# A linear-attention and channel-mix kernel rewritten on another tiling of its tokens

## The chip, the cores and the metric

The kernel runs on one core of one Trainium2 chip. A core has TensorE (matrix products, "PE"; its weight loads are listed apart as "PEld"), VectorE ("DVE"), ScalarE ("ACT"), GpSimd ("POOL") and SyncE ("SP"), which here only issues DMAs. The engines run side by side, each through its own list of instructions in order, and wait for each other by semaphores. SBUF is the working memory of 128 partitions, PSUM the memory that TensorE writes. The metric is the device time of one execution in microseconds (us), lower is better.

## What is computed

Four batches, four heads, 1,088 tokens, 32 features per head; r = 8. First an attention with a degree-2 sketch as its feature map, then a channel mix with d_model 128 and d_ff 1,024:

```python
def phi(x):                       # per token: 8 x 8 products
    a = np.einsum('rd,bhsd->bhsr', S1, x)
    b = np.einsum('rd,bhsd->bhsr', S2, x)
    return np.einsum('bhsi,bhsj->bhsij', a, b).reshape(*x.shape[:-1], r * r)
q_p, k_p = phi(q), phi(k)
kv = np.einsum('bhsf,bhsd->bhfd', k_p, v)
num = np.einsum('bhsf,bhfd->bhsd', q_p, kv)
den = np.einsum('bhsf,bhf->bhs', q_p, np.sum(k_p, axis=2))[..., None] + 1e-06
x = (num / den) with the heads side by side, (4, 1088, 128)

x_prev = x moved down by one token (zero first)
xk = mu_k * x + (1 - mu_k) * x_prev
xr = mu_r * x + (1 - mu_r) * x_prev
v = np.maximum(xk @ w_k, 0) ** 2 @ w_v
out = sigmoid(xr @ w_r) * v
```

Inputs and output are float32. The attention part is computed in float32, the channel mix in bfloat16 with float32 sums.

## The kernel before

A token is written 17 s + t, with s from 0 to 63 and t from 0 to 16. q, k and v of a batch are loaded by one DMA each from SP's queue (`load`, L120): two heads on the two halves of the 128 partitions, 64 values of s each, and for every partition and pair of heads 17 x 32 contiguous values. The weights come over GpSimd's queue (`w_load`, L215), two of them converted to bfloat16 by the DMA; mu_k and mu_r are loaded one value per partition.

Every task of the kernel is a small function, and one string, ORDER, lists them in the order in which they are issued; each engine takes its own instructions in that order. Numbers behind a name are batch or group, and part; a letter is the engine that does the copy or the product (A ScalarE, V VectorE). The tasks are:

- Attention, per batch, k side: transposes of k on TensorE (`t_pe`, L235) and their copies out of PSUM (`t_ev`); projections with S1 and S2 in four column strips of 32 (`kp_pe`, L252), their copy, and the 64 products per token and head (`kp_mul`, L273); sums over the tokens with v and of the projections themselves (`kv_pe`, L283), in 64-row tiles; their copy (`kv_cp`) and the forming of block-diagonal matrices (`kd_pe`, `kd_w`, `kd_ev`).
- Attention, per group of up to eight t (QG), q side: q is transposed in the same way; `q1_pe` (L355) projects it, together with a third product that gives the denominator; `q2` and `q2m` form denominator, quotient and the 64 products on VectorE; `q3_pe` and `q3_ev` transpose these; `q4_pe` (L408) multiplies by kv, which leaves x transposed (128 features by tokens) in PSUM.
- Channel mix: `q4_pp` writes (1 - mu_k) x to SBUF on ScalarE, `q4_xk` (L434) forms xk from it and from x in PSUM on VectorE, `q4_xb` writes x in bfloat16. `f1_pe` (L455) multiplies by w_k into two PSUM banks, `f1_act` is the relu on ScalarE (L464), `f1_sq` the square on VectorE (L470), `f2_pe` (L472) the product with w_v into the output's bank. `rr_pe` (L483) multiplies x and x_prev by w_r scaled by mu_r and by 1 - mu_r, two matmuls for every 128 tokens; `rr_act` is the sigmoid; `fin` (L498) the last product and the DMAs out.

Copies go through one helper, so in the profile they have the lines L196 (ScalarE) and L198 (VectorE), and are told apart by their tiles. Sixteen matmuls with zeros (L164) run at the very start. PSUM is given out by a pool with three names: two pairs of banks, three single banks and one for the output.

Of the kernel before, what the change touches and what calls it, by code (L numbers as in the profile page):

```python
# [64 lines left out]


# [482 lines left out]
```

## Time and profile before

| | us |
|---|---|
| runs | 119.43, 119.27, 117.3 |
| median of the runs | 119.27 |
| span of the profiled execution, first to last instruction | 115.9 |
| TensorE busy | 93.6 |
| TensorE weight loads busy | 72.1 |
| VectorE busy | 74.5 |
| ScalarE busy | 70.3 |
| GpSimd busy | 14.4 |

The profile shows the profiled execution by its span; its time as a run isn't listed beside it. The engine names in the rows are those given above, and a "q" behind one (SPq) is its instruction queue. A row of the list of groups reads: line, engine, operation, tile written <- tiles read, their shapes, how many; then busy us and mean ns of one; then how long the engine stood idle before them and who ended it. In the chain of waits (the work that ended last, followed back from the end), the three columns are the start, the length and what it was, with a count for consecutive ones. A row of sums by stage has the stage, its length, then for each engine busy us and number of instructions, then the clock that TensorE was granted as a share of full speed, the DMA engines' busy share and GB/s. Rows of the timeline have start, length, engine, line, operation and tiles.

### The profile page before, as it was taken

The numbers are of one execution on the slowest core, as the hardware profiler recorded it, in microseconds if no ns is written. First come the engines' busy times: TensorE is split into PE (matmuls) and PEld (weight loads), VectorE is DVE, ScalarE is ACT, GpSimd is POOL, SyncE is SP. The second block draws the span as 40 slices with busy tenths as digits, with TensorE's granted clock in tenths as the row PEclk, the third lists the DMA queues.
The fourth block names the chain that finished last, engine by engine and source line by source line (L and its number), as shares of the span: only waits on it lengthen the run. The fifth ranks groups of instructions, "written<-read, shape, count | busy, mean of one in ns | idle before, by whom it ended". The sixth has DMA issues, their size and how long they took to land.

```text
span 115.9 us, 5439 instructions
## 1 busy us (share of the span) xinstructions
PE 93.6 (81%) x2464; PEld 72.1 (62%) x2476; DVE 74.5 (64%) x149; ACT 70.3 (61%) x129; POOL 14.4 (12%) x47
## 2 busy tenths in 40 slices
PE   5995380794978996968877999899999999989820
PEld 2475270583867985667755888668858758667510
DVE  6128010269707939448637976979999999986820
ACT  4032230041629734737736997799999999999700
POOL 3059154000008000000002000100002300000000
PEclk9999999679999999999999999999999999999995
DMA  2999999900000000000020004021003011303213
GB/s 66 372 394 400 301 320 322 326 29 6 6 6 0 8 6 6 0 6 6 8 51 0 6 0 96 0 66 30 6 0 84 12 44 47 85 12 91 56 36 89
DMA packets 9317, 9.84 MB, mean 85 GB/s; under 512 B 1728, under 2 KB 6080, under 8 KB 9296
## 3 DMA queue, kind: packets, MB, share of 16 engines
q1 hardware_dynamic: 7984, 8.92, 24.1%
q0 software_dynamic: 1280, 0.59, 3.6%
q8 instruction: 19, 0.31, 1.1%
q14 instruction: 2, 0.02, 0.0%
q10 hardware_dynamic: 32, 0.00, 0.0%
HBM read 7.80 MB, written 2.23 MB: 87 GB/s over the span
## 4 chain that ended last, share of the span: by engine, by line
PE 73%; issue 13%; ACT 5%; DVE 3%; ACTq 1%; POOL 0%
PE o L479 11%; PE h L459 10%; PE x L416 9%; PE tp L243 8%; PE kv L294 7%; PE abw L366 6%; PE qt L399 6%; PE zeros L164 4%; PE abp L258 4%; PE r L491 3%; ACT k L464 2%; PE kv L301 2%; DVE kp L280 1%; ACTq L544 1%; PE kd L317 1%
## 5 line engine op out<-in xcount | busy, mean ns | idle before, releaser
L464 ACT ACTIVATE k<-h 128x1024 bf16<-128x1024 f32 (+1 forms) x36 | 35.0, 1002 | 1.8 <-PE h L459 1.2
L470 DVE TENSOR_TENSOR k<-k 128x1024 bf16<-128x1024 bf16 (+1 forms) x36 | 23.4, 656 | 2.2 <-ACT k L464 2.1
L479 PE MATMUL o<-wv,k 128*128 128x128 bf16 x272 | 20.8, 219 | 1.4 <-issue 0.7
L479 PEld LDWEIGHTS <-k 128*128 128x128 bf16 x272 | 17.1, 98 | 6.6 <-DVE k L470 1.4
L459 PE MATMUL h<-XK,wk 128*128 128x512 bf16 (+1 forms) x60 | 17.7, 364 | 1.0 <-DVE XK L438 0.4
L280 DVE TENSOR_TENSOR kp<-ab 128x1024 f32<-128x1024 f32 (+1 forms) x8 | 10.3, 1301 | 3.5 <-ACT ab L196 3.5
L301 PE MATMUL kv<-ab 64*32 64x16 f32 x272 | 9.5, 181 | 3.7 <-issue 3.7
L294 PE MATMUL kv<-kp,v 64*32 64x64 f32 x544 | 10.4, 225 | 2.0 <-DVE kp L280 1.2
L294 PEld LDWEIGHTS kv<-kp,v 64*32 64x32 f32 x544 | 8.5, 106 | 5.4 <-issue 3.1
L399 PE MATMUL qt<-ident,qp 128*128 128x128 f32 x68 | 10.6, 276 | 0.0
L393 DVE TENSOR_TENSOR qp<-an,abw 128x1024 f32<-128x1024 f32 (+2 forms) x9 | 10.4, 1159 | 0.1
L416 PE MATMUL x<-qpT,kvbd 128*32 128x256 f32 (+3 forms) x160 | 9.8, 351 | 0.8 <-issue 0.6
L301 PEld LDWEIGHTS kv<-ab 64*32 64x32 f32 x272 | 8.8, 106 | 1.9 <-issue 1.9
L429 POOL CAST XB<-X 128x63 bf16<-128x63 f32 x4 | 1.4, 343 | 64.2 <-ACT X L428 64.2
L366 PE MATMUL abw<-SQ,qT 128*32 128x96 f32 (+3 forms) x416 | 8.4, 228 | 1.0 <-issue 1.0
L432 ACT ACTIVATE PP<-x,omu_k 128x512 f32<-128x512 f32 (+7 forms) x12 | 6.7, 561 | 3.8 <-PE x L416 3.7
L366 PEld LDWEIGHTS abw<-SQ,qT 128*32 128x32 f32 x416 | 7.4, 116 | 2.3 <-issue 1.6
L399 PEld LDWEIGHTS qt<-ident,qp 128*128 128x128 f32 x68 | 7.7, 141 | 1.4 <-issue 0.2
L196 ACT COPY qpT<-qt 128x512 f32<-128x512 f32 (+2 forms) x15 | 8.4, 569 | 0.2 <-PE qt L399 0.2
L196 ACT COPY qT<-tp 128x512 f32<-128x512 f32 (+1 forms) x9 | 4.4, 494 | 6.4 <-PE tp L243 6.4
L438 DVE SCALAR_TENSOR_TENSOR XK<-x,mu_k,PP 128x512 bf16<-128x512 f32 (+7 forms) x12 | 6.8, 566 | 2.0 <-ACT PP L432 1.9
L198 DVE COPY kT<-tp 128x128 f32<-128x128 f32 (+1 forms) x5 | 2.2, 448 | 8.6 <-PE tp L243 8.6
(88 smaller groups left out, 142.2 us busy)
## 6 DMA issues: line engine op xcount, KB each, us to landing
k<-in_k_dram SPq DMA_DIRECT2D x4, 544.0 KB, 6.9
v<-in_v_dram SPq DMA_DIRECT2D x4, 544.0 KB, 10.3
q<-in_q_dram SPq DMA_DIRECT2D x4, 544.0 KB, 8.6
out_dram<-osb SPq DMA_DIRECT2D x11, 128.0 KB, 2.5
out_dram<-osb SPq DMA_DIRECT2D x4, 96.0 KB, 2.3
wk<-in_moe_w_k_dram POOLq DMA_DIRECT2D x1, 256.0 KB, 7.7
wv<-in_moe_w_v_dram POOLq DMA_DIRECT2D x1, 256.0 KB, 13.7
out_dram<-osb SPq DMA_DIRECT2D x4, 64.0 KB, 2.7
```

Source lines behind the costliest of these rows:

```text
L196: nc.scalar.copy(o, i)
L280: e.tensor_mul(kp[:, :n], _ap(a_, list(a_.ap[1:]) + [[0, R]]), _ap(b_, list(b_.ap[1:3]) + [[0, R]] + [b_.ap[3]]))
L294: nc.tensor.matmul(kv[32 * c:32 * c + 32, hh, :F], vin[b][rows, hp, t, :], kp[rows, t - t0, hp].rearrange("p i j -> p (i j)"), start=(t < ...
L301: nc.tensor.matmul(kv[32 * c:32 * c + 32, hh, F:F + 2 * R], ab[rows, t - t0].rearrange("p h x r -> p (h x r)"), ab[rows, t - t0, :, 1, :], ...
L366: nc.tensor.matmul(o[32 * c:32 * c + 32, i:i + n, hp, :] if n > 1 else o[32 * c:32 * c + 32, i, hp, :], xT["q", b][:, blk, 32 * c:32 * c + ...
L393: nc.vector.tensor_mul(qp[:, :n], _ap(a_, list(a_.ap[1:]) + [[0, R]]), _ap(b_, list(b_.ap[1:3]) + [[0, R]] + [b_.ap[3]]))
L399: nc.tensor.transpose(p[:, (i - 4 * hf) * P:(i - 4 * hf) * P + P], sb["qp", g][:, i].rearrange("p h i j -> p (h i j)"), ident[:])
L416: nc.tensor.matmul(p[32 * h:32 * h + 32, 64 * i0:64 * i1], kvbd[bs[i0]][:, hh, hp, :], r[:, i0:i1, 64 * hh:64 * hh + 64], skip_group_check ...
L459: nc.tensor.matmul(h[:, c, :n * 64], wk[:, (2 * cp + c) * P:(2 * cp + c + 1) * P], flat(XK, p0, n))
L464: nc.scalar.activation(k1[:, :, :n * 64], ps.pop(("h", g, cp))[:, :, :n * 64], RELU)
L470: nc.vector.tensor_mul(k2[:, :, :n * 64], k1[:, :, :n * 64], k1[:, :, :n * 64])
L479: nc.tensor.matmul(ps["o", g][:, i * P:i * P + P], k2[:, c, i * P:i * P + P], wv[:, 2 * cp + c, :], start=(cp == 0 and c == 0 and i == 0), ...
```

## The change

Nearly every task is rewritten, with the same mathematics:

- A token is written 34 a + u, with a from 0 to 31 and u from 0 to 33. The 128 partitions of q and k are now (head, a). Blocks of 32 x 32 are transposed on VectorE (`turn`), from SBUF to SBUF, which leaves (head, feature) on the partitions. Transposes of k and q on TensorE and their copies are gone.
- The projections take a whole 128 x 128 block of transposed tokens as the stationary operand (`kproj`, `abw`) and move block-diagonal S1 and S2. v is loaded in four pieces per batch, (u's quarter, a) on the partitions, and `kvmm` sums over 128 tokens at a time for each head.
- w_k, w_v and w_r are loaded in float32 on SP's queue and converted on GpSimd (`wset`); mu_k and mu_r are loaded as two rows and turned by a matmul. w_k and w_r are scaled by 1 - mu, and the mix becomes x mu / (1 - mu) + x_prev, so that x is copied out of PSUM once (`xev`), and r needs one matmul for 128 tokens instead of two; the r mix (`xr`) is done on GpSimd.
- Part of the k products (`kp.1.0`, `kp.3.0`, `kp.3.1`) and of the small products of the q side (`pw`, `an`) is on GpSimd; eight of the 36 squares are on ScalarE.
- Zero matmuls: five and five at the start, ten in seven places of the order (`zz`).
- PSUM is one tile of eight banks, and the order names the banks (behind @). The order itself is new throughout.

The core of the diff, without the removed functions:

```diff
+turn.k.0.0 wset.4 turn.k.0.1 wset.0 zz.1@0 kproj.0.1@0 kproj.0.0@1 abev.0.1.A turn.q.0.2 abev.0.0.A zz.2@0 zmm.0@0
+kp.0.1.V zev.0.A zz.1@7 wmm.0 wsq.0 kp.0.0.V zz.3@0 abw.0.1@0 abwt.0@1 abwev.0.1.A abw.0.0 turn.k.1.2 pw.0.18.34.G
+kvmm.0.0@0 abwev.0.0.A wset.1 kvmm.0.1 den.0.18.34 kproj.1.0@1 pw.0.0.18.G kvev.0.V an.0.18.34.G kproj.1.1@2
+den.0.0.18 abev.1.0.A kdmm.0 qp.0.1 abev.1.1.A an.0.0.18.G zz.1@1 zmm.1@1 kp.1.0.G zev.1.A qp.0.0 zz.1@7 wmm.1
+qt.0.1@23 qtev.0.1.A wsq.1 kvbm.0 zz.1@4 qtt.0@4 qt.0.0@56 kp.1.1.V qttev.0.A wset.3 xt.0 qtev.0.0.A kvmm.1.0@7
+turn.k.2.2 xmm.0.1@2 wset.2 xtev.0.A xs.0 turn.q.1.2 xmm.0.0@3 xev.0.1.A xr.0.2 kproj.2.1@5 xev.0.0.A xkt.0 turn.q.2.2
+abw.1.1@6 abev.2.1.A xr.0.0 abwt.1@5 abwev.1.1.A abw.1.0 xk.0.1 kproj.2.0@4 abwev.1.0.A xk.0.0 f1.1.1@01 xr.0.1
+abev.2.0.A kp.2.1.V rr.0@3 relu.1.1.A f1.0.0@56 zmm.2@2 kp.2.0.V kvmm.1.1 relu.0.0.A pw.1.0.34.G f1.1.0@01 rr.1@4
...
+    load_x(kin, k, 0, (slice(0, 1), slice(1, 2)))
+    load_x(qin, q, 0)
+    load_v(0)
+    load_x(kin, k, 1)
+    nc.sync.dma_start(wk_f[:, :, :DFF // 2], moe_w_k.rearrange("p (y f) -> p y f", y=2))
...
+    def turn(x, b, y):
+        n = U // 2 * D
+        for i in range(2):
+            if y in (i, 2):
+                if x == "k":
+                    nc.vector.transpose(_ap(kT[b % 2][:, 0, 2 * i], [[32, 2], [128, 9], [1, 32]]),
+                                        kin[b][:, i].rearrange("p (c m d) -> p c m d", c=2, m=9))
+                else:
+                    nc.vector.transpose(qT[b % 2][:, 17 * i:17 * i + 17, :].rearrange("p u a -> p (u a)"),
+                                        qin[b][:, i, :n])
+    def kproj(b, j, banks):
+        o = ps["ab", b, j] = PS[:, banks[0], :]
...
+            nc.tensor.matmul(_ap(d, [[n, 2], [1, 32]]), kT[b % 2][:, m].rearrange("p c a -> p (c a)"),
+                             SK[:].rearrange("p x h r -> p x (h r)"), skip_group_check=True)
+    def kvmm(b, j, banks=None):
...
+        for m in range(*KG[j]):
+            for h in range(H):
+                nc.tensor.matmul(o[32 * h:32 * h + 32, :F], vin[b][:, h, m, :],
+                                 sb["kp", b, j][:, 4 * (m - KG[j][0]) + h].rearrange("p i j -> p (i j)"),
+                                 start=(m == 0), stop=(m == 8), skip_group_check=True, tile_position=(0, 32 * h))
+    def xk(b, hf):
+        o = sb["xk", b, hf] = work.tile([P, 512], BF16, name="xk", tag="xk", bufs=4)
+        nc.vector.scalar_tensor_tensor(o[:], ps["x", b, hf], rat[:, :1],
+                                       X32[:, b % 2, 16 * hf:16 * hf + 16, :].rearrange("p u a -> p (u a)"),
+                                       op0=MUL, op1=ADD)
+    def xr(b, part):
...
+        nc.gpsimd.tensor_scalar(t[:, :n], x[:, u + 32:u + 32 + n], rat[:, 1:], 0.0, op0=MUL, op1=ADD)
...
+            nc.gpsimd.tensor_add(o[:], t[:], x[:, u:u + n])
+    def rr(g, banks):
...
+        for i in range(n):
+            nc.tensor.matmul(p[:, i * P:i * P + P], x[:, i * P:i * P + P], wr[:], skip_group_check=True)
     def fin(g):
...
+        for c in range(4):
+            rows = slice(32 * c, 32 * c + 32)
...
+            nc.sync.dma_start(dst, o[rows, :n // P, :])
```

The groups of the channel mix are now 512 tokens of one batch (16 values of u), two per batch, and a ninth one of 256 with the last two u of all four batches. `kdmm` is one transpose per batch, `zmm` and `wmm` give the denominator's weights, `qt` and `xmm` do what `q3_pe` and `q4_pe` did.

More of the change, by code (lines that the diff above doesn't have):

```diff
@@ L522 @@
+    for entry in ORDER.split():
+        task, _, banks = entry.partition("@")
+        name, *args = task.split(".")
+        args = [int(a) if a.isdigit() else a for a in args]
+        if banks:
+            args.append([int(i) for i in banks])
+        does[name](*args)
 _INS = ['q', 'k', 'v', 'S1', 'S2', 'moe_mu_k', 'moe_mu_r', 'moe_w_k', 'moe_w_v', 'moe_w_r']
```

679 lines of the change are left out of this document (303 added, 376 removed).

## The prediction

> **What bounds the kernel now.** I read the page's first line and its chain, then the list of the chain in order of time, then the sums by stage.
>
> ```profile
> PE 93.6 (81%) x2464; PEld 72.1 (62%) x2476; DVE 74.5 (64%) x149; ACT 70.3 (61%) x129; POOL 14.4 (12%) x47
> PE 73%; issue 13%; ACT 5%; DVE 3%; ACTq 1%; POOL 0%
> q8 instruction: 19, 0.31, 1.1%
> 12.74 1.99 issue
> 17.20 3.82 issue
> 27.44 1.73 issue
> 36.21 0.60 PE h L459 x4
> 110.93 0.69 DVE osb L502
> ```
>
> The chain that ended last runs through TensorE for 73% of the 115.9 us, and another 13%, 15.1 us, is "issue": the chain stands on an engine that waits for nothing the profile names. The other engines are on it for under 10%. The first matmul of the channel mix starts at 36.21, the last product ends at 110.93 + 0.69 = 111.62, and 4.2 us remain for the output to land.
>
> What the issue waits are is seen by counting TensorE's instructions up to each of the three longest:
>
> ```profile
> 0.00:12.74 12.74, 10.32 (x221) 6.35 (x222) 5.36 (x17) 3.83 (x8) 5.95 (x25) 1.00 0.85 312
> 0.00:17.20 17.20, 12.79 (x349) 8.53 (x349) 5.62 (x18) 5.06 (x10) 7.23 (x30) 1.00 0.92 308
> 0.00:27.44 27.44, 19.21 (x604) 13.89 (x604) 10.01 (x27) 7.11 (x16) 8.57 (x33) 0.94 0.84 268
> ```
>
> Matmuls and weight loads together make 443, 698 and 1208: 255 and 2 x 255 apart. The instruction queue moved 0.31 MB in 19 packets, and 4,940 TensorE instructions over 19 is 260. So I read the waits as TensorE coming to the end of a fetched block before the next is there; 15.1 us over 19 blocks is 0.8 us each. The kernel is bound by the number of TensorE's instructions as well as by their length.
>
> ```profile
> 36.20:60.00 23.80, 20.26 (x824) 16.79 (x829) 15.84 (x29) 13.41 (x28) 1.72 (x3) 1.00 0.03 8
> 60.00:80.00 20.00, 18.63 (x431) 14.99 (x429) 15.68 (x35) 16.94 (x33) 1.24 (x5) 1.00 0.13 31
> 80.00:105.00 25.00, 24.33 (x323) 17.59 (x326) 24.01 (x45) 24.33 (x38) 1.91 (x3) 1.00 0.15 35
> ```
>
> By stage (columns PE, PEld, DVE, ACT, POOL) TensorE is busy 85%, 93% and 97%; VectorE and ScalarE rise from 67% and 56% to 96% and 97%. So TensorE relieved alone gains in the first 80 us only; after that all three are full. The granted clock is 1.00 in all three.
>
> **TensorE after the change.** Rates from the chain, length over count:
>
> ```profile
> 80.14 0.44 PE qt L399 x4
> 79.69 0.45 PE o L479 x8
> 83.15 0.43 PE h L459 x2
> 84.83 1.07 PE x L416 x16
> 71.64 0.67 PE abw L366 x48
> 49.00 0.25 PE kv L294 x12
> 50.14 0.56 PE abp L258 x26
> 1.18 5.07 PE zeros L164 x16
> ```
>
> One f32 transpose is 0.11 us, an output matmul 0.056, a 512-wide one 0.215, an x instruction 0.067 at 256 columns, an abw 0.014, an abp 0.022; half a batch of kv, 96 instructions from 49.00 to 50.14, is 1.14, so 0.012 each. A plain f32 matmul shows as two instructions.
> - Gone: 72 transposes of k and q, 7.9; half of the 68 r matmuls, 1.9.
> - k projection: 320 instructions (6.9 us) become 72 with whole 128x128 weights. No row has this form; between the o row (0.056: 4.0) and the qt row (0.11: 7.9) I take 5, near the o row, as both move few columns.
> - kv and z: 816 (9.8) become 360 with four column strips. At the kv row 4.3, at twice that 8.6; I take 5.5.
> - q projection: 416 (5.8) become 96, 64 of them 96 wide; 5, an estimate by their columns.
> - kd: 192 become 12 instructions, about 2 to 0.9. x: 10 becomes 8.5. The qt transposes (7.5), f1 (14.7) and f2 (15.2) stay. Zeros: 16 become 20 (6.4 cold), the ten later ones in gaps.
>
> Sum, taken off the busy time: 93.6 becomes about 75, and 4,940 instructions become about 2,250: 9 blocks rather than 19, at 0.8 us 7 us of waits rather than 15. TensorE's line shrinks from 109 to 82 us, of which some 6 are zeros.
>
> **VectorE and ScalarE.**
>
> ```profile
> L470 DVE TENSOR_TENSOR k<-k 128x1024 bf16<-128x1024 bf16 x32 | 21.7, 685 | 2.2 <-ACT k L464 2.1
> L393 DVE TENSOR_TENSOR qp<-an,abw 128x1024 f32<-128x1024 f32 x7 | 8.5, 1218 | 0.0
> L502 DVE TENSOR_TENSOR osb<-o,r 128x512 f32<-128x512 f32 x8 | 5.5, 688 | 1.6 <-PE o L479 0.9 <-ACT r L496 0.7
> L438 DVE SCALAR_TENSOR_TENSOR XK<-x,mu_k,PP 128x512 bf16<-128x512 f32 x4 | 3.0, 744 | 0.0
> L198 DVE COPY qpT<-qt 128x512 f32<-128x512 f32 x3 | 2.0, 680 | 0.0
> L198 DVE COPY kT<-tp 128x128 f32<-128x128 f32 x3 | 0.9, 286 | 2.7 <-PE tp L243 2.7
> L464 ACT ACTIVATE k<-h 128x1024 bf16<-128x1024 f32 x32 | 32.8, 1051 | 1.8 <-PE h L459 1.2 <-PE x L416 0.3 <-PE kv L301 0.3
> L196 ACT COPY qpT<-qt 128x512 f32<-128x512 f32 x13 | 7.6, 596 | 0.2 <-PE qt L399 0.2
> ```
>
> The two copies give VectorE 154 ns + 1.03 ns per f32 element. The new VectorE transposes of 32x32 blocks stand in no row. I take the copy: 16 of 544 or 576 elements, 11.7 us; at the square's 0.5 ns 7, and at two passes 21 (an estimate: twice the copy's slope). [...]
>
> From the order: 28 squares on VectorE, four of them small, 18.2; 5 k products 6.6; 8 q products 10.2; xk and its tails 7.1; final products 5.9; 14 evictions 9.6; small ones, constants too, 10.2. With the transposes 79.5 us. Counted in this way (count times mean), before comes to 81.4, which overlap makes the 74.5 of the page; so 73 after. ScalarE keeps the 36 relus (36) and the sigmoids, takes 8 squares (8) and evictions, and loses PP, the copies of kT and qT and half of x: 67 against 81, so 59 busy against 70.
>
> **GpSimd.** It takes r's mix (24 instructions), 3 k products, part of the small products, and the scaling of the weights: about 16,000 elements per partition in 41 instructions.
>
> ```profile
> 17.92 0.39 POOL L233 COPY SQ<-SK 128x256 f32<-128x256 f32 x1
> 18.26 0.28 POOL L213 COPY klast<-k 128x128 f32<-128x128 f32 x1
> L229 POOL TENSOR_SCALAR wr_c<-wr_f,mu_r 128x128 bf16<-128x128 f32 x1 | 0.6, 609 | 0.1
> ```
>
> The copies give 0.9 ns an element and 0.17 fixed; the scaling, less the same 0.17, 3.4. So 21 to 61 us, and I take 2.1 ns, between them: 41 us, more than half idle. New waits hang on it. On VectorE den of batch 0 waits for a GpSimd product queued behind the scaling of w_k (1,024 elements, 1.1 to 3.7 us), and behind den wait qp and the turns of batch 2. On TensorE rr waits for xr, and f1 of a later group stands behind each rr. The five loads that leave its queue give 3 us back.
>
> **The front.** ```profile
> GB/s 66 372 394 400 301 320 322 326 29 6 6 6 0 8 6 6 0 6 6 8 51 0 6 0 96 0 66 30 6 0 84 12 44 47 85 12 91 56 36 89
> 0.73 0.44 SPq L123 DMA_DIRECT2D k<-in_k_dram  x1
> DMA to landing us min/median/max: 3.8/6.9/15.4
> ```
>
> SP's queue gets 28 loads instead of 12; at 0.44 us an issue that is 12.3 us, beside input that flows through the first eight of 40 slices, 23 us, and whose bytes don't change. q0 no longer stands behind v0. The first k lands 0.73 + 3.8 = 4.5 us in. Then VectorE in order: SK 5.6; two-part turn of k0, wset.4 and wset.0 to 8.6; q0 turned 10; two k products 12.8; turn of k1 14.3; den, the wait for the scaling 16.5; two qp 19.3; kp.1.1, turns of k2, q1, q2 25; xk 26.5. So f1 starts near 27, against 36.2: the two batches of turns are in it, the three issue waits and TensorE's transposes are not.
>
> **The sum.** By 27 VectorE has done 21 of its 73, so 52 remain; TensorE about 55 with its waits; ScalarE 51. Three nearly equal lines with GpSimd between them: before, the busiest engine was 92% busy from 36.2 to 105 (63.2 of 68.8). I take 85%, the lowest of the three stages: 61 us, so 88. Output 4.2, and 1 for the fourth DMA issue of the last products: span 93.5. The median of the runs, 119.27, stands 3.4 above the profiled span (the runs go from 1.4 to 3.6 above), and no time of the profiled execution itself is shown; I add 3.4: **97 us**. At 95% it is 90, at 75% 105.
>
> **Rivals.**
> 1. *VectorE and GpSimd shut each other out.*
>
> ```profile
> 36.20 1.29 POOL L213 COPY klast<-k 128x128 f32<-128x128 f32 x1
> 36.08 1.26 DVE L280 TENSOR_TENSOR kp<-ab 128x1024 f32<-128x1024 f32 x1
> 63.21 0.69 DVE L470 TENSOR_TENSOR k<-k 128x1024 bf16<-128x1024 bf16 x1
> 62.91 0.40 POOL L453 COPY XC<-XB 128x256 bf16<-128x256 bf16 x1
> ```
>
> A GpSimd copy of 0.28 takes 1.29 beside a product and ends 0.15 after it. The other way shows little: a square that starts 0.1 before a GpSimd copy ends takes its usual 0.69. If VectorE waits as well: 44 VectorE instructions with both inputs in SBUF meet a GpSimd that is busy 41 of some 77 us, half of a 1 us instruction each: 44 x 0.53 x 0.5 = 11.7 less what GpSimd yields, so +10: 107. [...]
>
> 2. *GpSimd becomes the bound (slower).* It starts near 11, waits some 10, then 41 x 0.17 + 16,000 p, then r, sigmoid, product 3, output 5.2, and 3.4. That is 39.6 + 16 p: over 121.7 from p = 5.1 ns, and 126 at 5.4. Against it: the dearest row is 3.4. For it: no f32 two-input row, and products with broadcast operands.
>
> 3. *The issue waits don't shrink* (it does not do what it says): blocks end at other places but cost the same 15.1 us: 8 on TensorE's line, 105.
>
> 4. *A tighter fit*: 95% or more, 90 or less.
>
> **How the numbers follow.** Forecast, 90 to 104: 0.56. Rival 1, 104 to 113: 0.20. Rival 2: 0.10. Rival 3: 0.06. Rival 4, down to 86: 0.08. The range 88 to 112 leaves out rival 2 and about half of rival 4, and takes in the dear end of the transposes (+9). No change means within 2%, 116.9 to 121.7, which is also about what a measurement of this kernel can tell. Faster 0.84 (all but rival 2 and the top of rival 1), within 0.05, slower 0.11.
>
> **What would show it.** Right: f1 starts near 27; transposes of 544 near 0.71; TensorE busy about 75 with some 2,250 instructions and issue under 8 us on the chain; VectorE above 80% from 27 on; chain spread over VectorE, ScalarE and TensorE. Wrong: squares and products beside GpSimd work stretched past their rows (rival 1); xr or the GpSimd k products at 3 us and rr waiting (rival 2); a start of f1 past 32.

## The result, and the profile after

| | before | after |
|---|---|---|
| runs, us | 119.43, 119.27, 118.2, 117.3 | 102.25, 102.22, 101.76, 104.45 |
| median, us | 118.73 | 102.23 |
| span of the profiled execution, us | 115.9 | 100.3 |

The ratio is 0.864, 95% interval 0.857 to 0.871: about 14% faster. The prediction was 97.0 with 88 to 112; the time is inside, 5.2 us above the point. The run of 104.45 was a disturbed one; such runs are left out of every ratio. The profiled execution is the one of 102.25, so 1.95 us lie around its span. Of the 15.6 us by which the span is shorter, 4.4 were won up to the first matmul of the channel mix, f1 (36.2 before, 31.8 after), and 12.9 from there to the end of the last product (75.4 before, 62.5 after); the output's tail lost 1.7 (4.3 before, 6.0 after).

The page of the changed kernel: busy times, the chain by engine, and the instruction queue.

```profile
PE 85.6 (85%) x1114; PEld 61.6 (61%) x1114; DVE 80.3 (80%) x128; ACT 60.4 (60%) x89; POOL 44.3 (44%) x70
q8 instruction: 8, 0.13, 0.5%
PE 30%; DMA 23%; DVE 23%; issue 9%; ACT 4%; POOL 3%; SPq 1%; DVEq 0%; POOLq 0%; ACTq 0%
```

TensorE has fallen from 73% of the chain to 30%, its instructions from 4,940 to 2,228, and the packets of the instruction queue from 19 to 8. Now the sums by stage (PE, PEld, DVE, ACT, POOL, then the granted clock), with the bounds that the prediction used for before:

```profile
10.00:20.00 10.00, 9.64 (x169) 7.50 (x169) 7.18 (x13) 2.59 (x7) 5.28 (x6) 1.00 1.09 248
20.00:27.00 7.00, 4.61 (x81) 2.55 (x78) 6.28 (x6) 3.15 (x6) 5.92 (x6) 1.00 1.08 266
27.00:36.20 9.20, 8.87 (x181) 7.07 (x182) 9.04 (x14) 6.02 (x12) 5.65 (x6) 1.00 0.81 178
36.20:60.00 23.80, 20.76 (x238) 15.49 (x232) 21.35 (x32) 20.11 (x27) 10.86 (x10) 1.00 0.09 25
60.00:80.00 20.00, 19.72 (x259) 14.02 (x258) 17.44 (x26) 13.73 (x19) 5.79 (x8) 0.92 0.10 28
```

From 27 us on no engine is the bound alone: VectorE is busy 98%, 90% and 87% of the three stages, TensorE 96%, 87% and 99%. Before, VectorE had 67% from 36 to 60. The chain changes engine all the time, which is what the small shares show.

**Where the 5.2 us of the miss lie.** Three rows of the timeline of the changed kernel (TensorE, VectorE, SP's queue) divide the span as the prediction had divided it:

```profile
31.77 0.59 PE L435 MATMUL ps<-xk,wk 128*128 128x512 bf16 x2
93.23 1.08 DVE L481 TENSOR_TENSOR osb<-ps,r 128x512 f32<-128x512 f32 x2
93.95 3.66 SPq L488 DMA_DIRECT2D out_dram<-osb  x8
```

| part | predicted | measured | difference |
|---|---|---|---|
| until the first f1 | 27 | 31.8 | +4.8 |
| from there to the end of the last product | 61 | 62.5 | +1.5 |
| to the end of the span | 5.2 (written as 5.5) | 6.0 | +0.5 |
| around the span | 3.4 | 1.95 | -1.5 |

The last product ends at 93.23 + 1.08 = 94.31. So nearly the whole miss of this execution is in the front; the same program, run again, had a front of 35.3 (next section). The second part came out close although two of its terms were off, as the next sections show.

### The profile page after: what moved, and what is told of

It is laid out like the page before. It is cut to its first block, busy times and chain, and to the rows that moved or that the text cites. A ratio compares the mean times of both kernels' runs of the same rounds, so it can differ in the third digit from the quotient of the medians.

```text
span 100.3 us, 2721 instructions
## 1 busy us (share of the span) xinstructions
PE 85.6 (85%) x1114; PEld 61.6 (61%) x1114; DVE 80.3 (80%) x128; ACT 60.4 (60%) x89; POOL 44.3 (44%) x70
## 4 chain that ended last, share of the span: by engine, by line
PE 30%; DMA 23%; DVE 23%; issue 9%; ACT 4%; POOL 3%; SPq 1%; DVEq 0%; POOLq 0%; ACTq 0%
DMA k<-in_k_dram 14%; DMA wk_f<-in_moe_w_k_dram 9%; DVE k L453 9%; PE ps L463 7%; PE ps L319 6%; PE ps L435 5%; PE ps L386 4%; ACT k L441 3%; DVE qp L355 2%; DVE qpT L224 2%; PE ps L245 2%; DVE xk L404 2%; PE ps L396 2%; PE ps L290 2%; POOL xrt L416 1%
## 5 line engine op out<-in xcount | busy, mean ns | idle before, releaser
L441 ACT ACTIVATE k<-ps 128x1024 bf16<-128x1024 f32 (+1 forms) x36 | 33.5, 984 | 2.6 <-PE ps L435 2.1
L463 PE MATMUL ps<-wv,k 128*128 128x128 bf16 x272 | 19.0, 219 | 2.1 <-DVE k L453 1.8
L435 PE MATMUL ps<-xk,wk 128*128 128x512 bf16 x64 | 17.7, 379 | 0.1
L355 DVE TENSOR_TENSOR qp<-an,abw 128x1024 f32<-128x1024 f32 (+1 forms) x8 | 12.4, 1548 | 0.3 <-POOL an L347 0.3
L416 POOL TENSOR_SCALAR xrt<-X,rat 128x512 f32<-128x512 f32 (+1 forms) x12 | 8.9, 743 | 5.4 <-DVE X L224 4.3
L421 POOL TENSOR_TENSOR xr<-xrt,X 128x512 bf16<-128x512 f32 x8 | 10.7, 1343 | 0.7
L245 PEld LDWEIGHTS ps<-SK,kT 128*128 128x128 f32 x72 | 9.2, 202 | 2.0 <-DVE kT L231 1.3
L386 PE MATMUL ps<-ident,qp 128*128 128x128 f32 x64 | 9.1, 290 | 0.9 <-DVE SQ L281 0.7
L245 PE MATMUL ps<-SK,kT 128*128 128x64 f32 x72 | 9.4, 283 | 0.4 <-DVE kT L231 0.4
L319 PE MATMUL ps<-SQ,qT 128*128 128x96 f32 x64 | 9.4, 296 | 0.1
```

The source lines that it names most:

```text
L245: nc.tensor.matmul(_ap(d, [[n, 2], [1, 32]]), kT[b % 2][:, m].rearrange("p c a -> p (c a)"), SK[:].rearrange("p x h r -> p x (h r)"), skip ...
L319: nc.tensor.matmul(o[:, c0 + 96 * t:c0 + 96 * t + 96], qT[b % 2][:, u:u + 4, :].rearrange("p u a -> p (u a)"), SQ[b][:].rearrange("p h r - ...
L355: nc.vector.tensor_mul(o[:, :s1 - s0], _ap(a_, list(a_.ap[1:]) + [[0, R]]), _ap(b_, [list(b_.ap[1]), [0, R], list(b_.ap[2])]))
L386: nc.tensor.transpose(o[:, p, t * P:t * P + P], sb["qp", b, hf][:, s:s + 2].rearrange("p s i j -> p (s i j)"), ident[:])
L416: nc.gpsimd.tensor_scalar(t[:, :n], x[:, u + 32:u + 32 + n], rat[:, 1:], 0.0, op0=MUL, op1=ADD)
L421: nc.gpsimd.tensor_add(o[:], t[:], x[:, u:u + n])
```

## The experiments

Each run stood beside runs of before on the same chip; their medians were 119.73 (e1 to e4), 119.01 (e5 to e8) and 118.65 (e9 to e12). "Front" is the start of the first f1, "middle" from there to the end of the last product, "tail" the rest of the span, all from the one profiled execution of each kernel, which isn't its median run.

| run | times, us | front | middle | tail | span |
|---|---|---|---|---|---|
| after | 102.25, 102.22, 101.76, 104.45 | 31.8 | 62.5 | 6.0 | 100.3 |
| e1_after_again | 104.62, 103.61, 107.27, 107.74 | 35.3 | 61.4 | 6.0 | 102.7 |
| e2_xr_memset | 97.56, 97.66, 97.75, 106.52 | 30.9 | 58.8 | 6.0 | 95.8 |
| e3_fin_tail | 103.97, 98.97, 100.96, 104.5 | 34.4 | 64.4 | 3.3 | 102.1 |
| e4_no_gap_zeros | 105.81, 104.7, 103.19, 105.14 | 35.0 | 63.1 | 6.0 | 104.0 |
| e5_warm | 103.12, 104.88, 103.09, 101.48 | 33.7 | 61.5 | 5.9 | 101.2 |
| e6_rr_two | 103.02, 100.87, 100.95, 103.95 | 32.7 | 62.0 | 6.4 | 101.1 |
| e7_v_two | 104.38, 104.07, 103.67, 103.19 | 32.1 | 64.4 | 5.5 | 102.0 |
| e8_all | 100.01, 98.67, 100.28, 97.18 | 32.7 | 62.0 | 3.2 | 97.9 |
| e10_r_on_vector | 101.1, 97.94, 103.92, 100.93 | 30.3 | 64.3 | 3.3 | 97.9 |
| e11_all_kp_back | 100.32, 97.04, 100.29, 101.12 | 32.6 | 62.0 | 3.2 | 97.8 |
| e12_squares | 102.49, 99.23, 102.07, 99.2 | 33.8 | 63.2 | 3.3 | 100.3 |

e9_before_less_z is a variant of the kernel before (116.51, one run). In after, e3, e4, e7 and e10 TensorE's clock fell in the middle, near 60 us, and in the others it did not (section on the clock); only middles of the same kind can be compared.

### The same kernel again, and without GpSimd's reads

The theory was that VectorE and GpSimd hold each other up (rival 1); against it, that the miss is a late start and a full middle. e1 is the changed kernel unchanged. e2 leaves out the r mix: its 24 GpSimd instructions only write zeros, so that they still stand in GpSimd's line but read nothing. They are also shorter: GpSimd is busy 31.1 us in e2 and 44.3 in the changed kernel.

```diff
-        nc.gpsimd.tensor_scalar(t[:, :n], x[:, u + 32:u + 32 + n], rat[:, 1:], 0.0, op0=MUL, op1=ADD)
+        nc.gpsimd.memset(t[:, :n], 0.0)
...
-            nc.gpsimd.tensor_add(o[:], t[:], x[:, u:u + n])
+            nc.gpsimd.memset(o[:], 0.0)
```

> The changed kernel as it is, on the same chip as the next three, so that they can be compared with it. Span near 100, time near 102, squares of 1,024 at 0.90 us, last product ends near 94.3, five to six microseconds before the end of the span.

> Leaves out the mix of r: each of the 24 GpSimd instructions of xr becomes a memset of the same tile, which writes SBUF and reads nothing, so r is the sigmoid of zero. Theory 1 (VectorE instructions with two SBUF inputs are held while GpSimd reads SBUF): the squares fall from 0.90 to 0.75 us or less, VectorE busy from 80.3 to 76 or less, the time falls by 3 to 5 us, to 97 to 99. Theory 2 (squares are slow for another reason, TensorE's 85.6 busy us set the time): squares stay above 0.85, the time falls by less than 1.5 us. Theory 3 (the lock is there, but what it costs is hidden behind TensorE): squares fall, the time falls by less than 1.5 us.

Measured: the ratio of e2 is 0.8165 (0.812 to 0.821), of e1 0.871 (0.863 to 0.878), of the changed kernel's first runs 0.864. So without the mix 5.7 us are gone against the first runs, 6.4 against e1. Not all of this is the lock, that is, the two engines shutting each other out: by the table, 4.4 of the difference to e1 stand in the front (30.9 for 35.3), where e1's TensorE is slow (below), and 2.6 in the middle (58.8 for 61.4), where neither profile has a fall of the clock. The lock itself is seen in the timeline of the changed kernel, the rows of VectorE first:

```profile
19.45 3.54 DVE L355 TENSOR_TENSOR qp<-an,abw 128x1152 f32<-128x1152 f32 x1 [0.32 <-POOL an L347]
50.94 1.79 DVE L453 TENSOR_TENSOR k<-k 128x1024 bf16<-128x1024 bf16 x1 [1.13 <-ACT k L441]
58.07 1.34 DVE L355 TENSOR_TENSOR qp<-an,abw 128x1152 f32<-128x1152 f32 x1
```

and of GpSimd:

```profile
19.38 2.40 POOL L259 TENSOR_TENSOR kp<-ab 128x1280 f32<-128x1280 f32 x1
50.91 1.27 POOL L421 TENSOR_TENSOR xr<-xrt,X 128x512 bf16<-128x512 f32 x1
```

The same product takes 3.54 us at 19.45 and 1.34 at 58.07. At 19.45 it began 0.07 us after a GpSimd product; that one ended at 21.78, the VectorE one at 22.99, 1.21 later: it waited out the whole GpSimd instruction and then did its work. The square at 50.94, 0.03 after an xr began, takes 1.79, where squares took 0.685 before. This is the order that no run had shown over 0.1 us when the prediction was made. How much it costs is read from the groups by form (mean ns of one is the number behind the busy time), first of the changed kernel:

```profile
L453 DVE TENSOR_TENSOR k<-k 128x1024 bf16<-128x1024 bf16 x24 | 21.1, 900 | 1.2 <-ACT k L441 1.1
L355 DVE TENSOR_TENSOR qp<-an,abw 128x1152 f32<-128x1152 f32 x4 | 7.6, 1895 | 0.3 <-POOL an L347 0.3
L259 DVE TENSOR_TENSOR kp<-ab 128x1024 f32<-128x1024 f32 x3 | 4.3, 1447 | 0.0
L259 DVE TENSOR_TENSOR kp<-ab 128x1280 f32<-128x1280 f32 x2 | 3.5, 1766 | 0.0
```

and of e2:

```profile
L453 DVE TENSOR_TENSOR k<-k 128x1024 bf16<-128x1024 bf16 x24 | 18.4, 786 | 1.6 <-ACT k L441 1.5
```

A square took 685 before. So the squares are stretched by 24 x 0.215 = 5.2 us, the products qp by 2.2 in the one instance, the kp by about 0.6 and 0.6 over their quiet lengths (1.26 in the row of before, 1.48 at 11.94): 8.6 us of VectorE in all, and 80.3 - 8.6 = 71.7 is the work without the lock. In e2 the squares keep 2.4 of their 5.2; one of 2.9 us still stands beside a GpSimd k product there. So the expected squares of 0.75 and VectorE at 76 us did not come: they are 0.786 and 77.4. VectorE's busy time falls by 2.9, close to the 2.6 us of the middle. How much of this is the lock and how much the shorter work of GpSimd, this run alone can't tell.

### The tail

The last products leave by eight DMAs, each issued from SP's queue behind the other. Against the theory that the landing sets the tail stood the theory that the issues do. e3 gives the last group one DMA in place of four, and issues two of the four of group 7 from ScalarE's queue.

```diff
-        for c in range(4):
+        for c in range(4 if g < 8 else 1):
...
-                dst = out[c].rearrange("(a u) f -> a u f", u=U)[:, 32:, :]
-            nc.sync.dma_start(dst, o[rows, :n // P, :])
+                rows = slice(0, P)
+                dst = out.rearrange("b (a u) f -> (b a) u f", u=U)[:, 32:, :]
+            q_ = nc.scalar if g == 7 and c > 1 else nc.sync
+            q_.dma_start(dst, o[rows, :n // P, :])
```

> The last group's output in one DMA instead of four, and two of the four of the group before it issued from ScalarE's queue. Theory A (the last 6 us are eight issues of 0.45 us in a row on SP's queue): from the last product to the end of the span 3.5 us instead of 6.0, the time falls by 2 to 2.5 us. Theory B (they are the landing of the last DMA and the end of the program): less than 0.7 us.

The timeline of e3, VectorE and then SP's queue, answers the rows of the changed kernel above:

```profile
97.71 1.08 DVE L481 TENSOR_TENSOR osb<-ps,r 128x512 f32<-128x512 f32 x2
98.43 1.29 SPq L490 DMA_DIRECT2D out_dram<-osb  x3
```

Three issues take 1.29 us where eight took 3.66, 0.43 to 0.46 each; the tail is 102.1 - 98.79 = 3.3 us instead of 6.0. So the issues set it, and they cost 2.7 us. The median of this run is no lower than that of the changed kernel (102.46; the lowest is 98.97): in the profiled execution front and middle were long, 34.4 and 64.4. e8, e10, e11 and e12 have the same short tail.

### TensorE's clock

e1 is the same program as the changed kernel and yet its first f1 starts at 35.3 rather than 31.8. The first 18 instructions of the k projection tell why; in the changed kernel, in e1 and in e5:

```profile
7.65 2.56 PE L245 MATMUL ps<-SK,kT 128*128 128x64 f32 x18
```

```profile
7.96 3.94 PE L245 MATMUL ps<-SK,kT 128*128 128x64 f32 x18
```

```profile
9.19 2.12 PE L245 MATMUL ps<-SK,kT 128*128 128x64 f32 x18
```

3.94 against 2.12 is a factor of 1.86. Where the profile of the changed kernel records the clock as down, 0.50 from 61 to 63 us, eight f32 projections of q take 1.88 us (from 61.57) and the next eight, with the clock back at 1.00, take 1.03 (from 63.40): a factor of 1.83. The column of the granted clock says 1.00 for the stage of the 18 in all three, so a half clock there is read from the lengths alone. The zeros of the start come in two bursts, 2.3 and 2.7 us long, with small matmuls and waits between them; before, 16 in a row took 5.07. e4 leaves out the ten zeros in the order, e5 makes the two bursts longer:

```diff
-turn.k.0.0 wset.4 turn.k.0.1 wset.0 zz.1@0 kproj.0.1@0 kproj.0.0@1 abev.0.1.A turn.q.0.2 abev.0.0.A zz.2@0 zmm.0@0
+turn.k.0.0 wset.4 turn.k.0.1 wset.0 kproj.0.1@0 kproj.0.0@1 abev.0.1.A turn.q.0.2 abev.0.0.A zmm.0@0
...
```

```diff
-    zz(5, [7])
+    zz(6, [7])
...
-    zz(5, [7])
+    zz(10, [7])
```

> The ten zero matmuls in the order are gone, the ten at the start stay. If they hold the clock up in the early gaps: the granted clock falls to 0.5 for some 3 us between 10 and 32 us and the time grows by 1 to 2 us. If they are of no use: granted clock unchanged, time within 0.7 us, or up to 1.5 us less, since they take 4 us of TensorE.

> Six zero matmuls instead of five before the small set-up products and ten instead of five behind them. In four executions of the changed kernel or of close kin, 18 f32 projections of batch 0 took 2.2 to 2.6 us twice and 3.9 to 4.0 us twice, with the same code: TensorE was at half clock until 18 to 24 us in the latter. Theory W (two bursts of 2.3 us do not surely wake the clock, 16 in a row before the change did): those 18 take 2.3 us in this run, the first matmul of the channel mix starts near 32 rather than 35, and the runs lie within 1.5 us of each other, at 101 to 103 us. Rival (the clock falls where it likes): spread of 3 us as before, 103 to 108.

In e5 TensorE runs at the faster rate from the first projection on (2.12 us), as expected, and pays for it: that projection starts 1.5 us later. But its times still spread over 3.4 us, which the longer bursts were to have ended, and the first f1 is at 33.7, since the clock fell again between 20 and 36 us (granted 0.91 and 0.89 there). So the slow start of TensorE is one cause of the late front and not the only one. Nor does the granted clock, as it is recorded, account for the whole spread: the four executions of e8, whose clock is 1.00 throughout (0.998 in one), have spans from 95.2 to 98.2; what makes these differ stays open. e4 has its clock down in the same stretch; its ratio, 0.869 (0.860 to 0.878), can't be told from e1's: what the zeros in the gaps are worth stays open.

There is also a fall in mid-kernel. Sums by stage of the changed kernel, ahead of it and in it:

```profile
56.70:59.60 2.90, 0.66 (x9) 0.52 (x10) 2.90 (x4) 2.10 (x3) 0.90 (x1) 1.00 0.00 0
60.20:63.60 3.40, 3.40 (x25) 2.95 (x24) 1.71 (x3) 0.00 (x0) 0.00 (x0) 0.56 0.02 5
```

TensorE, waiting for VectorE's held squares, does 0.66 us of work in 2.9, and then has a clock of 0.56 for 3.4 us. TensorE is full in these, VectorE half idle, ScalarE and GpSimd idle wholly, so what is lost is about 0.44 x 3.4 = 1.5 us (an estimate). e4 and e10 show the same fall, e3 and e7 a longer one (0.83 on average from 60 to 80 us in e7; in e3 three slices of 2.55 us at 0.5 to 0.7): the first eight transposes (qt) behind the wait take 1.76 us in the changed kernel and 1.53 in e10, and 1.06 in e2, e5 and e8. e1, e2, e5, e6, e8, e11 and e12 don't show it, although TensorE waits there too, e1 and e5 as long (TensorE's busy share in the two emptiest slices of some 2.5 us, in whole tenths: 0.5 and 0.4 from 55.2 to 60.2 in the changed kernel, 0.4 and 0.5 from 59.1 to 64.2 in e1, 0.6 and 0.3 from 55.7 to 60.7 in e5). The middles follow: with the r mix on GpSimd 61.4 and 61.5 without the fall (e1, e5), 62.5 to 64.4 with it. What decides when TensorE reaches its faster rate at the start and when its clock falls isn't shown: one projection took 2.56 and 3.94 us in two runs of one program, the 16 zeros of before took 5.07 us there and 6.30 in e9, which starts alike, and the fall came behind 2.9 us at 23% busy in some executions and not in others.

### The input

In the profiled execution of the changed kernel the input streams until about 34 us, where it took 23 before, and 23% of the chain is DMA (in e1, the same program, until 29, and 3%). Was the loading of v in pieces of 32 partitions the cause? e7 loads v with 64 partitions at a time, in half as many DMAs, on top of e5.

```diff
-        for c in range(4):
-            u, n = CU[c]
-            nc.sync.dma_start(vin[b][32 * c:32 * c + 32, :, :n, :].rearrange("p h m d -> p h (m d)"),
+        for z, (u, n) in enumerate(((0, 9), (9, 8))):
+            nc.sync.dma_start(vin[b][64 * z:64 * z + 64, :, :n, :].rearrange("p h m d -> p h (m d)"),
```

> As e5_warm, with v of a batch in two DMAs on 64 partitions instead of four on 32; rows stay 1,152 and 1,024 bytes. Theory P (DMAs on 32 partitions fill few engines): input ends near 26 us instead of 30 to 33, time 1 to 2 us less. Theory S (short rows): input ends where it did, time within 0.7 us.

The input ends near 31 us, not near 26 (29 in e5). The ratio is 0.875 (0.868 to 0.882), the lowest run 103.19 against 101.48 of e5, with a longer fall of the clock in the middle: no gain is seen. So the number of partitions in one DMA of v is not the cause. The short rows of v, which e7 keeps, and the weights, which now stand on the same queue between the inputs, are rivals that no run tried; why the input takes longer stays open. In the changed kernel VectorE waits for k and q for 0.7 and 1.0 us in all (groups by form):

```profile
L231 DVE STREAM_TRANSPOSE kT<-k 128x576 f32<-128x576 f32 x8 | 5.8, 756 | 0.7 <-DMA k<-in_k_dram 0.7
L234 DVE STREAM_TRANSPOSE qT<-q 128x544 f32<-128x544 f32 x8 | 5.4, 716 | 1.0 <-DMA q<-in_q_dram 1.0
```

So the share of DMA on the chain is mostly the loads' own length under a wait of 1.7 us; by VectorE's waits, earlier loads alone couldn't win more than that.

### Giving r's mix to other engines

If the lock costs what e2 gained, the mix should leave GpSimd. e6 (with e5's bursts) computes r by two matmuls, as before, with x copied to bfloat16 on ScalarE:

```diff
-        t = work.tile([P, 512], F32, name="xrt", tag="xrt", bufs=2)
-        nc.gpsimd.tensor_scalar(t[:, :n], x[:, u + 32:u + 32 + n], rat[:, 1:], 0.0, op0=MUL, op1=ADD)
...
-            nc.gpsimd.tensor_add(o[:], t[:], x[:, u:u + n])
+            nc.scalar.copy(XB[b][:, r0:r1, :].rearrange("p u a -> p (u a)"), x[:, r0:r1, :].rearrange("p u a -> p (u a)"))
...
-            nc.tensor.matmul(p[:, i * P:i * P + P], x[:, i * P:i * P + P], wr[:], skip_group_check=True)
+            for w, s0 in ((wr, 1), (wr_p, 0)):
...
+                nc.tensor.matmul(p[:, i * P:i * P + P], x, w[:], start=(i == 0 and s0 == 1), stop=(s0 == 0), skip_group_check=True)
```

e8 is e6 with e3's tail and e7's loads. e10 (e5's bursts, e3's tail) does the mix in one VectorE instruction for each piece:

```diff
-            nc.gpsimd.tensor_add(o[:], t[:], x[:, u:u + n])
+            nc.vector.scalar_tensor_tensor(o[:], x[:, u + 32:u + 32 + n], rat[:, 1:], x[:, u:u + n], op0=MUL, op1=ADD)
```

e11 is e8 with the GpSimd product that held qp at 19.4 moved to VectorE; e12 is e10 with four squares (2.1, 3.3, 4.2, 5.2) moved to ScalarE:

```diff
-kp.1.0.G
+kp.1.0.V
```

```diff
-sq.2.1.V
+sq.2.1.A
...
```

> As e5_warm, and the r mix leaves GpSimd: ScalarE copies x to bfloat16, and TensorE multiplies x and x_prev by two scaled copies of w_r, as before the change (34 matmuls of 0.056 more, 12 copies of 0.3 to 0.6 us on ScalarE, 24 GpSimd instructions less). Theory 1 (the lock): squares of 1,024 at 0.80 or less, 3.5 to 6 us less than e5_warm, near 97. Rival (GpSimd's share is worth it, ScalarE or TensorE is full): within 1 us of e5_warm or slower.

> e5_warm with the r mix of e6_rr_two, the loads of v of e7_v_two and the output of e3_fin_tail. If the three gains add (5, 1 and 2.5 us): 94 us. If the lock's gain is all behind one of the others: 97 or more.

> The r mix on VectorE, one instruction for each of the 12 pieces (about 7 us more for it), none on GpSimd; start as in e5_warm, output as in e3_fin_tail. Theory 1 with a full VectorE: squares at 0.77, VectorE busy 81 to 84 as in the changed kernel, the time that of the changed kernel less the 2.7 us of the output: 99 to 101; what the lock cost and what the mix costs on VectorE cancel. If TensorE alone sets the time: 97, as it is rid of the 34 matmuls of e6_rr_two and of nothing else.

> e8_all with the first GpSimd k product (kp.1.0) back on VectorE. In the changed kernel's profile a q product beside it took 3.54 us instead of 1.35 (19.45 to 22.99, the k product ended at 21.78). Theory 1: that wait of 2.2 us goes, VectorE does 1.5 more, the first matmul of the channel mix starts 0.5 to 1 us earlier, time 0 to 1 us less than e8_all. Rival (GpSimd's help is worth its lock): later by 1.5.

> e10_r_on_vector with four more squares on ScalarE (1.06 us there for 0.69 on VectorE), in the stage where ScalarE is 70% busy. If VectorE sets that stage: 1 to 2 us less than e10. If TensorE sets it: within 0.5.

The lock goes: a square's mean falls to 770 in e6 and 774 in e10. The time hardly does. e6 (ratio 0.851, 0.843 to 0.858) is 1.1 us under e5 by the medians (101.99, 103.11) and 0.6 by the lowest runs (100.87, 101.48). The medians of e8, e10, e11 and e12 are 99.34, 101.02, 100.31 and 100.65, with spreads of 3 to 6 us, the lowest runs 97.18, 97.94, 97.04 and 99.20; most of what they gain on the changed kernel is the tail's 2.7. The middle is what the mix bears on. Where the clock didn't fall in it, it is 62.0 us in e6, e8 and e11 and 63.2 in e12, against 61.4 and 61.5 with the lock (e1, e5); with the fall it is 64.3 in e10, against 62.5 to 64.4. Only e2, where nobody does the mix, has 58.8. So e8's gains did not add up to 94, and e12's four squares bought nothing that can be seen (ratio 0.840, 0.833 to 0.847). The stage sums of e8 point to the reason:

```profile
36.20:60.00 23.80, 21.69 (x303) 16.40 (x304) 20.05 (x33) 21.42 (x32) 5.54 (x4) 1.00 0.09 24
60.00:80.00 20.00, 19.46 (x278) 14.27 (x281) 17.81 (x29) 16.20 (x24) 1.08 (x3) 1.00 0.13 35
```

VectorE is down by 1.3 us in the first of these stages against the changed kernel, and ScalarE is up by 1.3, TensorE by 0.9 to 91%, then 97%. In e10 the group of the mix shows the price on VectorE:

```profile
L420 DVE SCALAR_TENSOR_TENSOR xr<-X,rat 128x512 bf16<-128x512 f32 x8 | 6.0, 748 | 0.4 <-POOL X L377 0.4
```

6.0 us, more than the 3 us by which its squares are shorter; VectorE is busy 82.6 us there, in the 81 to 84 expected (the times, 97.9 to 103.9, fit both of its theories). So the lock is a real cost on VectorE, and GpSimd is no worse a place for the mix than the two others that were tried. In e11 the first f1 starts at 32.55, in e8 at 32.65, not 0.5 to 1 us earlier: on VectorE the k product (about 1.7 us) stands ahead of qp, which is still held beside other GpSimd work (about 2.2 for 1.34; the four of this length have a mean of 1.558). e8 has the lowest median, 99.34, a ratio of 0.835 by medians and without an interval; by the ratios that is 3 to 4 us under the changed kernel.

### What the issue waits of before were

The prediction read them as the ends of fetched blocks, every 255 TensorE instructions. e9 takes the kernel before and leaves out the sums for the denominators over all but the last four t, 416 TensorE instructions. If the count sets the waits, they stay at 443 + 255 k of the remaining ones; if the place in the program does, they stay with their operations.

```diff
-            for hh in range(2):
+            for hh in range(2 if t >= T - 4 else 0):
```

> The kernel before, which leaves out the sums of the projections (the denominators' weights) for all but the last four of the 17 t of each batch: 416 TensorE instructions less. Theory F (the issue waits come every 255 matmuls and weight loads, where a fetched block ends): the long waits again stand at counts of 443, 698, 1208 or at other steps of 255 from there, give or take 4, though other work stands there now (143 instructions further on by the third batch's k side at 698). Rival (they belong to the work or to the input's transfer: kv and kd of batch 0 and 1): the waits stay before the same instructions, kv and kd of batch 0, at counts lower by 52 to 104.

Sums from the start of e9's span to the beginning of six of its issue waits (first two counts: matmuls and weight loads):

```profile
0.00:13.95 13.95, 11.53 (x221) 6.55 (x222) 5.37 (x17) 4.16 (x8) 5.95 (x25) 1.00 0.85 320
0.00:21.36 21.36, 16.34 (x349) 10.49 (x349) 6.79 (x20) 5.32 (x11) 8.56 (x33) 0.92 0.95 315
0.00:25.62 25.62, 19.10 (x476) 12.74 (x476) 8.88 (x24) 6.81 (x16) 8.56 (x33) 0.93 0.89 286
0.00:32.25 32.25, 24.41 (x730) 17.31 (x731) 13.50 (x32) 10.15 (x26) 8.56 (x33) 0.95 0.71 228
0.00:42.55 42.55, 32.82 (x984) 24.41 (x985) 20.04 (x45) 16.16 (x39) 10.03 (x39) 0.96 0.54 174
0.00:48.74 48.74, 38.18 (x1237) 28.68 (x1239) 24.59 (x53) 20.69 (x46) 10.03 (x39) 0.96 0.48 153
```

443, 698, 952, 1461, 1969, 2476, where 443 + 255 k gives 443, 698, 953, 1463, 1973, 2483 (a few records are missing in a trace). Up to 60 us two more waits of over 0.6 us stand at 1,205 (for 1,208) and 2,986 (for 2,993); one of 0.22 at 2,601 doesn't fit. At 698 the wait now stands ahead of a projection (abp, L258), where it stood ahead of a kd matmul, and the count is the same: the count it is. That a fetched block ends there is a reading of these counts and of the instruction queue, which moved 18 packets instead of 19. The changed kernel, with 8, has no issue wait in the list of TensorE's matmuls at all; its weight loads have some, each 0.4 us or shorter but for one of 0.8, and none of TensorE's is among the longer pieces of the chain (the issue time there stands on the other engines, 5.8 of its 8.6 us on GpSimd). So 15.1 us on the chain became about nothing, not the 7 I had left. Why the ends of the remaining blocks cost nothing isn't shown; matmuls last longer there, 85.6 us for 1,114 against 93.6 for 2,464.

## Why the prediction was right, and where it was wrong

**Right: TensorE was the bound, by the count of its instructions too.** The issue waits went (rival 3 fell), and the chain spread over the engines, as "What would show it" had it. No run takes the rewriting apart, so how the 15.6 us are shared among its parts isn't shown. **Right in size:** VectorE's work, 80.3 less the 8.6 of the lock, 71.7 for 73; the new transposes at the copy's price, 0.716 us for 544 (0.71 said); ScalarE 60.4 for 59; GpSimd 44.3 for 41.

**Rival 2 fell.** GpSimd's products, of the changed kernel by form:

```profile
L259 POOL TENSOR_TENSOR kp<-ab 128x1280 f32<-128x1280 f32 x2 | 5.2, 2620 | 0.0
L416 POOL TENSOR_SCALAR xrt<-X,rat 128x512 f32<-128x512 f32 x8 | 5.5, 692 | 5.4 <-DVE X L224 4.3 <-ACT X L222 1.1
L421 POOL TENSOR_TENSOR xr<-xrt,X 128x512 bf16<-128x512 f32 x8 | 10.7, 1343 | 0.7
```

2,620 for 1,280 is 2.0 ns an element, 2.1 was taken; 5.1 would have been needed.

**Wrong, the step "the front": 27 became 31.8.** The prediction had the two products qp done at 19.3; they were done at 22.99. 2.2 of these 3.7 us are the hold shown above, which stood in rival 1 and was left out of the forecast. The other 1.5 were lost before qp: the turn of k1 ended 0.5 late, and two waits of VectorE follow it in the changed kernel (total, times, longest), 1.0 more than the step had allowed:

```profile
DVE kvs L224 <- PE ps L290: 0.9, 1, 0.9
DVE den L339 <- POOL pw L333: 0.8, 1, 0.8
```

The first wait wasn't in the step, the one behind den was named in it. But the chain to the first f1 doesn't lead through qp in this execution. It is:

```profile
14.14 11.52 DMA k<-in_k_dram
25.68 1.44 DVE kT L231 x2
27.12 1.26 DVE qT L234 x2
28.43 1.13 PE ps L319 x8
29.56 0.22 PE ps L308 x8
29.79 1.06 PE ps L319 x8
30.85 1.09 PE ps L245 x10
31.94 0.43 PE ps L435 x2
```

By the prediction's line the turn of k2 would have started near 20.6 (19.3 and a k product of 1.3). k2 landed only just ahead of its start at 25.68, 5.1 us later; this alone would make up the 4.8. The prediction let the turn of k2 wait for no DMA. With its hold VectorE came there at 24.96 and waited 0.7; without it, it would have waited longer for the same k2. Nor did f1 follow xk, as the prediction had it: the first xk was done by 30.7, and TensorE went through 34 projections without a gap from 28.43 on before it came to f1. In e2, e5 and e8, where VectorE doesn't wait for k2, the chain to the first f1 leads through the held qp (3.55 us) and then through TensorE; in e1 it stands on TensorE almost from the start. So there are several paths of nearly one length, by the run, and taking the hold off one of them bought nothing in e11. What the hold costs the front is not shown. The prediction went by VectorE alone, without the landing of k2, TensorE's line and its clock.

**Rival 1 is half true.** It put the lock at +10: 11.7 us on VectorE less what GpSimd yields. VectorE is held for 8.6 us, and in the time e2, without the mix, shows 2.6 us less in the middle. The sign that was named for it, products stretched past their rows, is there; the forecast had taken none of it. It came out near by luck, because the remaining work ran denser: from 31.77 to 94.31 VectorE is busy 57.1 of 62.5 us, 91%, not the 85% that I took from the lowest stage of before. At 85% the 57.1 would have been 67: +6 from the hold, -4.6 from a fuller line, two errors that nearly cancel in the term of 61.

**Wrong in size: TensorE, 75 became 85.6.** The forms with a whole 128 x 128 f32 block as weights:

```profile
L245 PE MATMUL ps<-SK,kT 128*128 128x64 f32 x72 | 9.4, 283 | 0.4 <-DVE kT L231 0.4
L319 PE MATMUL ps<-SQ,qT 128*128 128x96 f32 x64 | 9.4, 296 | 0.1
L386 PE MATMUL ps<-ident,qp 128*128 128x128 f32 x64 | 9.1, 290 | 0.9 <-DVE SQ L281 0.7
```

The chain to the first f1, above, has ten of the first (1.09 us) and eight of the second (1.13): 0.109 us an instruction with 64 columns and 0.14 with 96, where a transpose with 128 has 0.11: moving fewer columns gained nothing. I had taken the k projection near the output's bf16 row (5 of 4.0 to 7.9) because both move few columns; it is at the other end, and the q projection too, which had no upper bound in the text. By these rates the k projection is 7.8 us and the q projection 9.9 (with its 32 narrow instructions, 0.22 for eight); by the groups they are 9.4 and 10.6, where 5 each was taken: 8 to 10 of the 10.6. The zeros (8.0 for 6.4) are 1.6 more. What this cost in time isn't shown; TensorE was no longer the bound alone.

**Small:** the tail took 6.0 for 5.2 (eight issues in a row; I had counted 1 us for one more), and 1.95 lie around the span, not 3.4. That these two partly cancel is luck.

## What to carry to other kernels

When work moves to an engine that can hold up a full one, as GpSimd does VectorE here (8.6 us in all), put the hold into the forecast itself: count the pairs that can meet, and look in the trace for the same instruction at two lengths. When one engine stops being the bound and others are nearly as full, taking 3 us of delay off one of them buys little, because the work must still go somewhere; a variant that leaves it out gives the ceiling, not the gain. For a start, follow every engine's line and the landing of every input, not the one line that looks longest. And divide the time of a prediction into front, middle and tail: here the terms erred in both directions, and only the division shows which of them were right.

## What the runs showed of the hardware that was not expected

- VectorE waited out a whole GpSimd instruction of 2.40 us that began 0.07 us earlier, and then did its own work: 3.54 us for a product of 1.34.
- The matmuls of f32 with a 128 x 128 block of weights took some 0.11 us or more per listed instruction: 0.109 with 64 columns, 0.14 with 96, 0.11 with 128.
- TensorE's clock: behind the same two bursts of zeros, 2.3 and 2.7 us long, 18 instructions took 2.56 or 3.94 us in two runs of one program, under a recorded clock of 1.00; and behind 2.9 us at 23% busy the recorded clock fell to 0.56 for 3.4 us, in some executions of one kind and not in others.
- The issue waits follow the count of TensorE's instructions (443 + 255 k) in two programs; in the kernel before they cost up to 3.8 us each, in the changed kernel nothing that the chain shows.
- DMA issues on one queue stand 0.43 to 0.46 us apart, and eight of them made more than half of the tail.
